# Row-tiled feed-forward products, a new order of the slot and two gates of eight on GpSimd, in a kernel of thresholded attention and a gated feed-forward layer

## The chip, the cores and the metric

The kernel runs on one core of one Trainium2 chip. The metric is the device time of one execution in microseconds (us). Before the change it is 562.9 us, the median of three runs (561.4 to 563.7).

The engines in the profile are PE (TensorE, matmuls), PEld (its weight loads), DVE (VectorE), ACT (ScalarE), POOL (GpSimd) and SP (DMA queues). A "q" behind an engine's name means its sequencer, the part that takes instructions in order.

## The reference

```python
# q, k, v: (8, 8, 576, 64) f32; w_in: (512, 2048); w_out: (2048, 512)
scores = scale * np.matmul(q, k.transpose(0, 1, 3, 2))
thresh = np.max(scores, axis=-1, keepdims=True) - tau
scores = np.where(scores >= thresh, scores, -1000000000.0)
...                                          # softmax of what is left: attn
x = np.matmul(attn, v)                       # then (4608, 512)
h = x @ w_in
g = h * np.clip(h + 3.0, 0.0, 6.0) / 6.0     # the gate
out = g @ w_out
```

## The kernel before

Sixteen groups of four heads are worked through in nine slots each, 144 slots in all. In a slot VectorE takes 128 rows of scores of two heads out of the accumulators and finds each row's maximum. GpSimd turns the maximum into a bias, ScalarE masks with that bias and later exponentiates, and GpSimd normalises. Between these stand pieces of the feed-forward layer of an earlier batch: an input product (512 to 2048 wide, two blocks of 128 at a time), its gate, and a quarter of an output product. The code below is condensed; `...` marks what is left out.

```python
    def sm_max(sl):
        ...
        for i, ps in enumerate(sl.tiles):
            nc.vector.tensor_scalar(out=sl.s[:, i, :]..., in0=ps[:, :, 0:HALF],
                                    scalar1=1.0, scalar2=None, op0=Alu.mult, op1=Alu.max,
                                    accum_out=sl.m[:, i:i + 1])
            nc.gpsimd.tensor_scalar(out=sl.bias[:, i:i + 1], in0=sl.m[:, i:i + 1], scalar1=-scale, scalar2=tau,
                                    op0=Alu.mult, op1=Alu.add)
    ...
    def sm_norm(sl):
        for i in range(2):
            nc.gpsimd.tensor_scalar(out=pn[:, i, :], in0=sl.s[:, i, :], scalar1=sl.rinv[:, i:i + 1], scalar2=1.0,
                                    op0=Alu.mult, op1=Alu.mult)
    ...
    def mm1(item, pool=None):                        # input product: full 128 rows
        for n in range(2):
            for ki in range(KI):
                nc.tensor.matmul(hps[:, n, 0:w], w_in_sb[:, ki, (ni + n) * P:(ni + n + 1) * P],
                                 xT[b][:, ki, c0:c0 + w], start=(ki == 0), stop=(ki == KI - 1))
    def mm1_relu(hps, on_act):                       # max(h + 3, 0), on ScalarE or VectorE
    def mm1_gate(item, hps, r):                      # min(r, 6) * h, on VectorE
    ...
    # one slot
        sm_exp(prev, 0); sm_exp(prev, 1)
        sm_max(sl)
        h = mm1(item)
        r = mm1_relu(h, on_act=(slot in (0, 1, 3, 5)))
        mm1_gate(item, h, r)
        ...                                          # a quarter of an output product
        sm_mask(sl, 0); sm_mask(sl, 1)
        ...                                          # transposes, or attention times values
        queue[n + 1].tiles = scores(...)             # the next slot's scores
        sm_norm(prev)
```

The input product has one pair of accumulator banks (`ps_h`, bufs=1). The gate of a slot frees it for the next slot's product.

Of the kernel before, what the change touches and what calls it, by code (L numbers as in the profile page):

```python
# [21 lines left out]
def kernel(  # L22
# [21 lines left out]
    N2 = 28  # L44
# [13 lines left out]
    r_pool = ctx.enter_context(tc.tile_pool(name="rp", bufs=2))  # L58
    g_pool = ctx.enter_context(tc.tile_pool(name="gp", bufs=1))
# [4 lines left out]
    ps_m = ctx.enter_context(tc.psum_pool(name="ps_m", bufs=1))  # L64
# [126 lines left out]
    def bank(name):  # L191
        nonlocal turn
        turn += 1
        if now < N2 and turn % 2:
            return ps_o.tile([P, 512], F32, tag="o", name=name)
        return ps_m.tile([P, 512], F32, tag="m", name=name)
# [12 lines left out]
    def main_pe(src, pair):  # L209
        ps = bank("tp")  # L210
        n = pair % 2
        for t in range(4):
            nc.tensor.transpose(ps[:, t * P:(t + 1) * P], src[:, t, 2 * n:2 * n + 2, :], identf[:])  # L213
        return ps

    def transpose_q(pair):
        nq = nat[pair // 2][0]
        if by_pe(pair):
            ps = main_pe(nq[:, 0:1024].rearrange("p (t h d) -> p t h d", h=4, t=4), pair)
            return lambda: nc.vector.tensor_copy(out=qT_of(pair)[:, 0:512], in_=ps[:])  # L220
        n = pair % 2
        nc.vector.transpose(out=qT_of(pair), in_=nq[:, n * S:(n + 1) * S])

    def transpose_k(pair):
        ps = main_pe(nat[pair // 2][1], pair)
        return lambda: copy_out(kT_of(pair)[:, 64:576], ps[:])

    def transpose_rest(quad):
        ps = bank("tr")
        nq, _, kr = nat[quad]  # L230
        nc.tensor.transpose(ps[:, 0:P], kr[:], identf[:])
        if by_pe(2 * quad):
            nc.tensor.transpose(ps[:, P:2 * P], nq[:, 1024:1152], identf[:])

        def evict():
            qT, kT = qkT[quad]
            both = ps[:].rearrange("p (w n t) -> p w n t", n=2, t=64)
            if by_pe(2 * quad):
                nc.vector.tensor_copy(out=qT[:, :, 512:S], in_=both[:, 1])
            copy_out(kT[0:64, :, S:S + 64], both[0:64, 0])  # L240
            copy_out(kT[64:P, :, 0:64], both[64:P, 0])
        return evict
# [7 lines left out]
    def scores(quad, slot):  # L250
        tiles = [ps_s.tile([P, 2, 512], F32, tag="s", name="s") for _ in range(2)]
        for hf in range(2):
            if slot < 8:
                pair, t = 2 * quad + slot // 4, slot % 4
                for a in range(2):
                    nc.tensor.matmul(tiles[a][:, hf, 0:HALF], qT_of(pair)[a * 64:(a + 1) * 64, t * P:(t + 1) * P],  # L256
                                     keys(pair, a, hf), start=True, stop=True)
            else:
                for n in range(2):
                    for a in range(2):  # L260
                        pair = 2 * quad + n
                        nc.tensor.matmul(tiles[a][n * 64:(n + 1) * 64, hf, 0:HALF],  # L262
                                         qT_of(pair)[a * 64:(a + 1) * 64, 512:S], keys(pair, a, hf),
                                         start=True, stop=True)
        return tiles
# [4 lines left out]
    def sm_max(sl):  # L270
        sl.s = s_pool.tile([P, 2, S], F32, tag="s", name="s")
        sl.m = stat_pool.tile([P, 2], F32, tag="m", name="m")
        sl.bias = stat_pool.tile([P, 2], F32, tag="bias", name="bias")
        sl.rsum = stat_pool.tile([P, 2], F32, tag="rsum", name="rsum")
        sl.rinv = stat_pool.tile([P, 2], F32, tag="rinv", name="rinv")
        for i, ps in enumerate(sl.tiles):
            nc.vector.tensor_scalar(out=sl.s[:, i, :].rearrange("p (a b) -> p a b", a=2), in0=ps[:, :, 0:HALF],  # L277
                                    scalar1=1.0, scalar2=None, op0=Alu.mult, op1=Alu.max,
                                    accum_out=sl.m[:, i:i + 1])
            nc.gpsimd.tensor_scalar(out=sl.bias[:, i:i + 1], in0=sl.m[:, i:i + 1], scalar1=-scale, scalar2=tau,  # L280
                                    op0=Alu.mult, op1=Alu.add)
# [36 lines left out]
    def av(ps, pair, pT, cols):  # L318
        b, hp = divmod(pair, NPAIR)
        vm, vr = vsb[b]  # L320
        for c in range(4):
            for a in range(2):
                nc.tensor.matmul(ps[a * 64:(a + 1) * 64, :], vm[:, 2 * hp + a, c * D:(c + 1) * D],  # L323
                                 pT[:, 5 * a + c, cols], start=(c == 0), stop=False)
# [3 lines left out]
    def av_main(pair):  # L328
# [3 lines left out]
        ps = bank("av")  # L332
        av(ps[:], pair, pts[pair], slice(0, 512))
        o0 = 64 if b % 2 else 0
        nc.vector.tensor_copy(out=xT[b][:, hp, o0:o0 + 512], in_=ps[:])  # L335

    def av_rest(quad):
        b, g = divmod(quad, 2)
        ps = bank("ar")
        for n in range(2):  # L340
            av(ps[:, n * 64:(n + 1) * 64], 2 * quad + n, ptr[quad], slice(n * 64, (n + 1) * 64))
        o0 = 0 if b % 2 else 512
        nc.vector.tensor_copy(out=xT[b][:, 2 * g:2 * g + 2, o0:o0 + 64],
                              in_=ps[:, 0:P].rearrange("p (a b) -> p a b", a=2))
# [3 lines left out]
    def mm1(item, pool=None):  # L348
# [6 lines left out]
        return hps[:, :, 0:w]  # L355

# [16 lines left out]
    o_ps = {}  # L373

    def mm2_part(bb, mt, part, pool=None):
        if part == 0:
            if pool:
                o_ps[0] = pool.tile([P, 2, 512], F32, tag="s", name="o")[:, 0, :]
            else:
                o_ps[0] = ps_o.tile([P, d_model], F32, tag="o", name="o")[:]  # L380
        for ni in range(part * 4, part * 4 + 4):
            nc.tensor.matmul(o_ps[0], gbuf[:, ni, mt * P:(mt + 1) * P], w_out_sb[:, ni, :],  # L382
                             start=(ni == 0), stop=(ni == NI - 1))

    def mm2_out(bb, mt, on_act):
        osb = o_pool.tile([P, d_model], F32, tag="osb", name="osb")
        if on_act:
            nc.scalar.activation(out=osb[:], in_=o_ps[0], func=Act.Copy, scale=1.0 / 6.0)  # L388
        else:
            nc.vector.tensor_scalar_mul(out=osb[:], in0=o_ps[0], scalar1=1.0 / 6.0)  # L390
# [16 lines left out]
    def moe_of(b):  # L407
        items = []
        for c0, w, mts in (((0, 320, (4, 5, 6)), (320, 256, (7, 8))) if b % 2 else
# [3 lines left out]
            items[-1] = (items[-1][0], [(b // 2, mt, part) for mt in mts for part in range(4)])  # L413
# [19 lines left out]
    prev = None  # L433
    for n, sl in enumerate(queue):
# [11 lines left out]
        if slot == 0 and g == 1 and b + 1 < B:  # L446
            load_v(b + 1)
        if prev is not None:
            for i in range(2):
                sm_exp(prev, i)  # L450
        sm_max(sl)

        if slot != 8 and todo1:
            item, then = todo1.pop(0)
            h = mm1(item)
            r = mm1_relu(h, on_act=(slot in (0, 1, 3, 5)))
            mm1_gate(item, h, r)
            todo2.extend(then)
        copies = pe_transpose(queue[n - 2]) if n > 1 and queue[n - 2].on_chip else None
        if prev is not None:  # L460
            sm_recip(prev)
        if copies:
            copies()
        outs = []


        pieces = 0 if slot == 3 else 1
        if slot == 0:
            second = True
        if second and slot < 2 and len(todo2) > 1 and todo2[0][1] == todo2[1][1]:  # L470
            pieces, second = 2, False
        for _ in range(pieces):
            if todo2:
                bb, mt, part = todo2.pop(0)
                mm2_part(bb, mt, part)
                if part == 3:
                    outs += mm2_out(bb, mt, on_act=False)
        for i in range(2):
            sm_mask(sl, i)
        evict = None  # L480
        nxt = 2 * quad + 2
        if slot == (1 if quad else 2):
            evict = transpose_q(2 * quad + 1)
        elif slot == (2 if quad else 3):
            evict = transpose_k(2 * quad + 1)
        elif slot == 3 and quad > 0:
            av_main(2 * quad - 1)
        elif slot == 4 and quad > 0:
            av_rest(quad - 1)
            if quad % 2 == 0:  # L490
                todo1.extend(moe_of(quad // 2 - 1))
        elif slot in (5, 6, 7) and quad + 1 < NQUAD:
            if slot == 5:
                alloc_qk(quad + 1)
                evict = transpose_q(nxt)
            elif slot == 6:
                evict = transpose_k(nxt)
            else:
                evict = transpose_rest(quad + 1)
        elif slot == 8:  # L500
            av_main(2 * quad)
        if evict:
            evict()
# [4 lines left out]
        if prev is not None:  # L508
            sm_norm(prev)
        flush()  # L510
# [23 lines left out]
    def rest2():  # L534
        while todo2:
            bb, mt, part = todo2.pop(0)
            mm2_part(bb, mt, part, pool=ps_s if count[1] % 3 else None)
            if part == 3:
                flush()
                late.extend(mm2_out(bb, mt, on_act=(count[1] % 2 == 0)))  # L540
                count[1] += 1
# [3 lines left out]
    av_main(2 * last + 1)  # L545
    rest2()
    av_rest(last)
# [38 lines left out]
```

## Time and profile before

| before | value | how to read it |
|---|---|---|
| time | 562.9 us | median of 3 runs |
| nine slots in the loop from slot 27 on | 31.5 us | from the starts of the row maxima, slots 36 to 135 |
| end of the loop to end of the program | 60 us | from the last slot's first maximum at 502.5 us |

The prediction below shows the main lines and the engines' shares in the loop. These are three more of the page's groups of instructions, which matter for the argument about GpSimd. The columns are line, engine, operation, names, shapes and count, then busy time in us and the mean ns of one, then the idle time before.

```profile
L298 POOL TENSOR_SCALAR pn<-s,rinv 128x576 bf16<-128x576 f32 x288 | 211.6, 745 | 133.5 <-issue 58.5
...
L280 POOL TENSOR_SCALAR bias<-m 128x1 f32<-128x1 f32 x288 | 54.4, 189 | 69.0 <-DVE s L277 48.2
...
L364 DVE TENSOR_SCALAR r<-h 128x512 f32<-128x512 f32 (+1 forms) x54 | 40.5, 751 | 0.0
```

The normalisation is the only large GpSimd operation. It takes 0.745 us for 576 elements a partition. On VectorE the add-and-maximum of the gate (L364) takes 0.75 us.

### The profile page before, as it was taken

To read this page: it belongs to the slowest core of one execution; us is meant where nothing else is said; L and a number is where in the kernel's file an instruction comes from. 1 tells how busy PE (TensorE), PEld (TensorE's weight loads), DVE (VectorE), ACT (ScalarE), POOL (GpSimd) and SP (SyncE) were. 2 spreads that over 40 slices of the span, in tenths; PEclk is the share of its full clock that TensorE was granted. 3 is DMA by queue.
4 is the path that set the end of the run, shared out by engine and by line. 5 is a ranking of instruction groups with operands and counts; after the bars stand their busy time and mean duration, and the time that the engine had idled before them with its cause. 6 is when DMAs were issued, how large, how long until landed. Compare 5 with 4: busy or idle time off the path is not lost.

```text
span 562.3 us, 11634 instructions
## 1 busy us (share of the span) xinstructions
PE 535.0 (95%) x3856; PEld 309.3 (55%) x3856; DVE 424.4 (75%) x1040; ACT 470.3 (84%) x999; POOL 305.2 (54%) x646
## 2 busy tenths in 40 slices
PE   7998798899999999999999999999999999999997
PEld 5665455455545565555555565655555565654663
DVE  3588787687878788787878798887978798883440
ACT  4799899798988999989898999899898999983540
POOL 1678878854556555655456555755556555561000
PEclk8899999899999999999999999999999999999999
DMA  5879999997689876978589867987699865453102
GB/s 110 135 110 166 162 160 184 207 148 144 112 159 153 151 153 127 208 139 155 114 150 170 159 137 146 174 160 146 127 137 175 167 124 117 101 109 86 38 20 75
DMA packets 286204, 77.52 MB, mean 138 GB/s; under 512 B 269248, under 2 KB 281536, under 8 KB 286144
## 3 DMA queue, kind: packets, MB, share of 16 engines
q1 hardware_dynamic: 268736, 67.86, 64.8%
q0 software_dynamic: 17408, 8.92, 13.7%
q8 instruction: 30, 0.49, 0.4%
q14 instruction: 30, 0.25, 0.2%
HBM read 36.70 MB, written 9.44 MB: 82 GB/s over the span
## 4 chain that ended last, share of the span: by engine, by line
PE 58%; DVE 11%; ACT 9%; issue 4%; POOL 1%; DMA 1%; SPq 1%; DVEq 0%; POOLq 0%
PE h L353 18%; PE o L382 17%; PE s L256 16%; DVE s L277 5%; ACT s L285 4%; PE av L323 3%; ACT s L290 3%; DVE g L370 2%; DVE r L364 2%; ACT r L362 2%; PE s L262 1%; PE tp L213 1%; PE ar L323 1%; DVE osb L390 1%; POOL pn L298 1%
## 5 line engine op out<-in xcount | busy, mean ns | idle before, releaser
L298 POOL TENSOR_SCALAR pn<-s,rinv 128x576 bf16<-128x576 f32 x288 | 211.6, 745 | 133.5 <-issue 58.5
L277 DVE TENSOR_SCALAR_CACHE_REDUCE s<-s 128x576 f32<-128x576 f32 x288 | 205.9, 752 | 44.9 <-PE s L256 35.2
L285 ACT ACTIVATE s<-s,bias 128x576 f32<-128x576 f32 x288 | 207.1, 766 | 36.8 <-POOL bias L280 35.7
L290 ACT ACTIVATE s<-s 128x576 f32<-128x576 f32 x288 | 192.7, 671 | 0.3
L256 PE MATMUL s<-kT,qT 64*128 64x288 f32 x1024 | 172.7, 435 | 5.4 <-DVE s L277 3.2
L353 PE MATMUL h<-xT,w_in_sb 128*128 128x320 bf16 (+1 forms) x1024 | 145.0, 287 | 5.5 <-DVE g L370 4.6
L382 PE MATMUL o<-w_out_sb,g 128*128 128x512 bf16 x576 | 140.9, 379 | 3.6 <-DVE osb L390 3.0
L353 PEld LDWEIGHTS <-w_in_sb 128*128 128x128 bf16 x1024 | 92.0, 97 | 68.4 <-issue 31.1
L256 PEld LDWEIGHTS s<-kT,qT 64*128 64x128 f32 x1024 | 94.8, 188 | 62.7 <-DVE s L277 24.9
L370 DVE SCALAR_TENSOR_TENSOR g<-r,h 128x512 bf16<-128x512 f32 (+1 forms) x128 | 96.4, 754 | 41.2 <-ACT r L362 39.3
L280 POOL TENSOR_SCALAR bias<-m 128x1 f32<-128x1 f32 x288 | 54.4, 189 | 69.0 <-DVE s L277 48.2
L382 PEld LDWEIGHTS <-g 128*128 128x128 bf16 x576 | 55.6, 98 | 58.2 <-issue 9.8
L362 ACT ACTIVATE r<-h,three 128x640 f32<-128x640 f32 (+1 forms) x74 | 54.4, 737 | 21.1 <-PE h L353 20.4
L290 ACT ACTIVATION_READ_ACCUMULATOR s<-s 128x1 f32 x288 | 54.2, 188 | 0.0
L364 DVE TENSOR_SCALAR r<-h 128x512 f32<-128x512 f32 (+1 forms) x54 | 40.5, 751 | 0.0
L390 DVE TENSOR_SCALAR osb<-o 128x512 f32<-128x512 f32 x31 | 21.0, 676 | 22.2 <-PE o L382 22.2
L323 PE MATMUL av<-pT,vm 128*64 128x512 bf16 x256 | 34.6, 392 | 2.0 <-ACT kT L203 2.0
L323 PEld LDWEIGHTS <-vm 128*64 128x64 bf16 x512 | 18.1, 111 | 25.2 <-issue 18.3
L293 DVE RECIPROCAL rinv<-rsum 128x2 f32<-128x2 f32 x144 | 23.0, 160 | 10.2 <-ACT s L290 9.5
L335 DVE CAST xT<-av 128x512 bf16<-128x512 f32 x32 | 21.8, 681 | 5.6 <-PE av L326 5.3
L277 DVE DVE_READ_ACCUMULATOR s<-s 128x1 f32 x288 | 23.9, 83 | 0.0
L388 ACT ACTIVATE osb<-o 128x512 f32<-128x512 f32 x5 | 3.0, 597 | 23.9 <-PE o L382 23.9
(42 smaller groups left out, 255.9 us busy)
## 6 DMA issues: line engine op xcount, KB each, us to landing
km<-in_k_dram SPq DMA_DIRECT2D x64, 128.0 KB, 3.0
out_dram<-osb SPq DMA_DIRECT2D x32, 256.0 KB, 2.4
nq<-in_q_dram SPq DMA_DIRECT2D x96, 72.0 KB, 2.7
vm<-in_v_dram POOLq DMA_DIRECT2D x16, 256.0 KB, 5.4
nq<-in_q_dram SPq DMA_DIRECT2D x16, 128.0 KB, 3.9
w_in_sb<-in_moe_w_in_dram POOLq DMA_DIRECT2D x16, 128.0 KB, 4.1
w_out_sb<-in_moe_w_out_dram POOLq DMA_DIRECT2D x16, 128.0 KB, 4.5
pT<-pn SPq DMA_TRANSPOSE x119, 3.4
```

What stands on the lines that cost most here:

```text
L256: nc.tensor.matmul(tiles[a][:, hf, 0:HALF], qT_of(pair)[a * 64:(a + 1) * 64, t * P:(t + 1) * P], keys(pair, a, hf), start=True, stop=True)
L277: nc.vector.tensor_scalar(out=sl.s[:, i, :].rearrange("p (a b) -> p a b", a=2), in0=ps[:, :, 0:HALF], scalar1=1.0, scalar2=None, op0=Alu.m ...
L280: nc.gpsimd.tensor_scalar(out=sl.bias[:, i:i + 1], in0=sl.m[:, i:i + 1], scalar1=-scale, scalar2=tau, op0=Alu.mult, op1=Alu.add)
L285: nc.scalar.activation(out=s, in_=s, func=Act.Prelu, bias=sl.bias[:, i:i + 1], scale=scale, alpha=REJECT)
L290: nc.scalar.activation(out=s, in_=s, func=Act.Exp, accum_out=sl.rsum[:, i:i + 1])
L298: nc.gpsimd.tensor_scalar(out=pn[:, i, :], in0=sl.s[:, i, :], scalar1=sl.rinv[:, i:i + 1], scalar2=1.0, op0=Alu.mult, op1=Alu.mult)
L323: nc.tensor.matmul(ps[a * 64:(a + 1) * 64, :], vm[:, 2 * hp + a, c * D:(c + 1) * D], pT[:, 5 * a + c, cols], start=(c == 0), stop=False)
L353: nc.tensor.matmul(hps[:, n, 0:w], w_in_sb[:, ki, (ni + n) * P:(ni + n + 1) * P], xT[b][:, ki, c0:c0 + w], start=(ki == 0), stop=(ki == KI ...
L362: nc.scalar.activation(out=r, in_=hps, func=Act.Relu, bias=three[:])
L364: nc.vector.tensor_scalar(out=r, in0=hps, scalar1=3.0, scalar2=0.0, op0=Alu.add, op1=Alu.max)
L370: nc.vector.scalar_tensor_tensor(out=gbuf[:, ni:ni + 2, c0:c0 + w], in0=r, scalar=6.0, in1=hps, op0=Alu.min, op1=Alu.mult)
L382: nc.tensor.matmul(o_ps[0], gbuf[:, ni, mt * P:(mt + 1) * P], w_out_sb[:, ni, :], start=(ni == 0), stop=(ni == NI - 1))
```

## The change

Its intent: from slot 27 on, the input and output products run as pairs of 64-row tiles, so that TensorE need not switch its tiling between them and the scores. The two tiles write two banks and exchange them halfway; a VectorE nop between the two phases keeps them apart. Keys of four heads are transposed in one slot, token tiles of the output are spread over six slots, and of the eight gates of a group GpSimd takes two and ScalarE's relu two. The cut-out is condensed, with comments added.

```diff
-    N2 = 28
+    N2 = 27
+    ACT_RELU, POOL_GATE = (3, 6), (2, 5)
-    ps_m = ctx.enter_context(tc.psum_pool(name="ps_m", bufs=1))
...
+    class Banks:
+        def products(self, phase, insts):
+            follows(insts[0], self)
+            if self.phase not in (None, phase):
+                relay = nc.vector.nop(nofuse=True)
+                tc.add_manual_dep(relay.ins, self.after.ins.name, SYNC, reason="end of a phase")
+                tc.add_manual_dep(insts[0].ins, relay.ins.name, SYNC, reason="next phase")
+            self.phase, self.after = phase, None
...
+    def mm1_phase(item, hps, phase):
+        for ki in range(KI):
+            for a in range(2):
+                n, c = a ^ phase, row_tile(a)
+                insts.append(nc.tensor.matmul(
+                    hps[:, n, 0:w], w_in_sb[c, ki, (ni + n) * P:(ni + n + 1) * P], xT[b][c, ki, c0:c0 + w],
+                    start=(phase == 0 and ki == 0), stop=(phase == 1 and ki == KI - 1)))
+        h_banks.products(phase, insts)
...
+    def mm1_gate_pool(item, hs):
+        nc.gpsimd.tensor_scalar(out=r, in0=hs, scalar1=3.0, scalar2=0.0, op0=Alu.add, op1=Alu.max)
+        nc.gpsimd.tensor_scalar(out=r, in0=r, scalar1=6.0, scalar2=1.0, op0=Alu.min, op1=Alu.mult)
+        nc.gpsimd.tensor_tensor(out=gbuf[:, ni:ni + 2, c0:c0 + w], in0=r, in1=hs, op=Alu.mult)
...
     # one slot, from slot 27 on
+            if phase or nis.stop < NI:
+                parts = [(one, phase, nis[:4]), (one, phase, nis[4:])]
+        sm_max(sl, 0)
+                mm1_phase(item, h, 0)
+                mm2_phase(*parts[0][0], *parts[0][1:])
+                mm1_phase(item, h, 1)
+                mm2_phase(*parts[1][0], *parts[1][1:])
         sm_exp(prev, 0); sm_exp(prev, 1)
+        sm_max(sl, 1)
+        sm_mask(sl, 0)
+            if slot in by[1]:
+                hs = mm1_copy(h)
+                gate = lambda: mm1_gate_pool(item, hs)
+            else:
+                mm1_gate(item, h, mm1_relu(h, on_act=slot in by[0]))
+        sm_mask(sl, 1)
...
         sm_norm(prev)
+        if gate:
+            gate()
```

The GpSimd gate is emitted at the end of its slot, so it stands in GpSimd's order directly ahead of the next slot's two biases.

## The prediction

> **What bounds the kernel now.** I read the page first: engine shares, slices, the chain of waits.
>
> ```profile
> PE 535.0 (95%) x3856; PEld 309.3 (55%) x3856; DVE 424.4 (75%) x1040; ACT 470.3 (84%) x999; POOL 305.2 (54%) x646
> ...
> PE   7998798899999999999999999999999999999997
> ...
> PE 58%; DVE 11%; ACT 9%; issue 4%; POOL 1%; DMA 1%; SPq 1%; DVEq 0%; POOLq 0%
> ```
>
> TensorE is busy nearly everywhere after the first sixth and carries most of the chain. The change touches the loop from slot 27 of 144 on, so next came the busy times of that stretch, then those of the tail:
>
> ```profile
> 98.60:501.10 402.50, 393.64 (x2887) 224.66 (x2886) 332.52 (x814) 364.88 (x787) 230.62 (x488) 1.00 0.83 147
> ...
> 520.00:540.00 20.00, 19.77 (x164) 14.28 (x163) 11.53 (x16) 11.71 (x16) 0.00 (x0) 1.00 0.08 28
> ```
>
> The columns are length, then PE, weight loads, DVE, ACT, POOL, clock, DMA. In the loop TensorE is at 98%, ACT at 91%, DVE at 83%, POOL at 57%. The tail (after 501 us, 61 us) is all TensorE and the change leaves its arithmetic alone. But a busy PE need not be streaming, so I looked at TensorE's timeline for one slot:
>
> ```profile
> 307.11 1.24 PE L256 MATMUL s<-kT,qT 64*128 64x288 f32 x8
> 308.38 1.03 PE L353 MATMUL h<-xT,w_in_sb 128*128 128x256 bf16 x8
> 309.25 1.03 PE L382 MATMUL o<-w_out_sb,g 128*128 128x512 bf16 x4
> 310.11 0.60 PE L213 MATMUL tp<-identf,km 128*128 128x128 f32 x4
> 310.64 1.24 PE L256 MATMUL s<-kT,qT 64*128 64x288 f32 x8
> ```
>
> Scores run in two 64-row tiles, everything else on 128 rows. From the starts of single matmuls in the trace (between 110 and 500 us) the steady rates are: a pair of score matmuls every 0.242 us, 0.109 or 0.136 us for an input product of 256 or 320 columns, 0.216 us for an output product, 0.109 us for a transpose. Around the scores these rates are broken. Going into them takes 0.309 us after an output product instead of 0.216, and their second pair follows 0.346 us after the first instead of 0.242, for its weights were not loaded ahead: about 0.19 us together. Leaving them takes 0.335 us (median; mean 0.374) instead of 0.242: about 0.13 us. So a round trip costs 0.32 us, nine times in a group of four heads.
>
> As a check: groups 5 to 14 start at 167.2 us and end at 481.1, 31.4 us each. Streaming is scores 8 x 4 x 0.242 + 4 x 0.242 = 8.7; input products 64 x 0.1225 = 7.8; output products 2.25 x 16 x 0.216 = 7.8; attention times values 10 x 0.216 + 0.3 = 2.5; transposes 9 x 0.109 = 1.0. Sum 27.8. Nine round trips add 2.9, three entries into the values' column tiles 0.3. That is 31.0 of 31.4: TensorE sets the pace, and tiling switches are 10% of it.
>
> The waits between engines show what stands close behind:
>
> ```profile
> DVE g L370 <- ACT r L362: 39.3, 72, 3.4
> ACT s L285 <- POOL bias L280: 35.7, 72, 1.9
> DVE s L277 <- PE s L256: 35.2, 53, 2.8
> ...
> PE h L353 <- DVE g L370: 4.6, 11, 0.7
> ```
>
> VectorE is the one that waits for the scores; TensorE waits for the gates only 4.6 us in all.
>
> **What the Trainium skill says.** "TensorEngine Tiling (Array Packing)", Tiling Modes, Key Properties: changing the tiling mode drains TensorE. The trace agrees (0.09 us extra into the scores, 0.09 out, before weights). The same page, Gotcha 1: different row tiles must not access one PSUM bank at the same time, and software has to see to it. That is the reason for the phases; no trace here shows it. "Perfetto Trace Analysis", Per-engine timelines: a sequencer-only instruction performs its wait in the sequencer, before the next is fetched. In the trace a VectorE event wait before the row maximum passes 0.035 to 0.042 us after the modelled end of the scores, and later ones follow only then. "GPSIMD Engine Reference", Elementwise: a two-input operation takes about 2.6 cycles an element.
>
> **The change, part by part, for one group of nine slots.**
>
> Row-tiled products. Each 128-row product becomes two 64-row ones that run beside each other into two banks, as the scores' pairs do, so I keep 0.109 and 0.136 us a pair and no gain in streaming. What goes is switching: slots 1 to 7 get their scores straight after row-tiled work (slot 8's own 64x64 scores, the last transposes and the values still switch). That is 7 x 0.19 = 1.3 us off; the seven departures would be 7 x 0.13 = 0.9 us more. Slot 4 now has values between two phases, +0.2.
>
> Phase waits. In phase 1 each row tile writes the bank that the other wrote in phase 0. Before it a VectorE nop must see the first foreign product after phase 0 finish, and TensorE waits for the nop. But the helper's remembered phase is never cleared for the input products: phase 0 of the next slot also differs from the last phase 1, so it gets a nop too, and that nop stands in VectorE's order behind the first row maximum, which waits for these very scores. So the input product cannot follow the scores directly. Counted from the last score pair's start: its end at 0.402, the event passes at 0.44, event and the maximum's two instructions about 0.14 (four such dispatches take 0.24 between two event waits), the nop some 0.05 (an estimate from event records of 0.02 to 0.05), back to TensorE 0.055 (an output bank's release at 315.436 to its matmul at 315.49), weights 0.096. Sum 0.78 against 0.242 streaming: 0.5 us of idle TensorE, where leaving used to cost 0.13. Eight slots with a product: 8 x 0.37 = +3.0. The phase-1 nop costs little: from the end of phase 0 it needs 0.27 (first product's latency) + 0.04 + 0.05 + 0.055 + 0.096 = 0.51, and four output pairs fill 0.44: +0.07 in five slots, +0.35. It also holds back the second row maximum by about 0.4 us, VectorE time that then presses on the next gate.
>
> Sum: -1.3 + 0.2 + 3.0 + 0.35 - 0.1 (one entry less for values) = +2.1 us a group, 13 groups: +28 us. Had the phase-0 nop been free, it would be -1.3 - 0.9 + 0.2 + 0.35 - 0.1 = -1.7, so -23 us.
>
> Keys in one slot. Eight transposes become 16 of 64 rows, two at a time: same time, no switch, counted above. Token tiles over six slots: the same products, in halves of 16 x 0.109 = 1.75 us; VectorE and ACT get uneven slots, which costs a little where a short slot follows.
>
> ACT and GpSimd. ACT loses two relus of four, 2 x 0.62 (start to start) = 1.2 us of some 28 us; VectorE trades two gates (0.67 each) for two copies of the same size. GpSimd gets two gates: two operations of about 0.745 us (the page's row for 576 elements) and one two-input at 576 x 2.6 / 1.2 GHz = 1.25 us, an estimate from the page, 2.7 us each. 57% becomes about 75%. The ACT relief is worth something only if TensorE stops being the bound.
>
> **Rivals.** (1) The switches were the bound and the waits hide: 27.8 us streaming, six switches left; ACT (26.7 us a group) and VectorE (25.5) come close behind, and 29 to 30 us a group would give 535 to 545 us. For it: the arithmetic of before closes with switches alone, and a change with so many matched parts has probably been tried out. Against it: the nop behind the row maximum. (2) The nop's idle time replaces the switches, 575 to 595 us, as summed. For it: VectorE demonstrably passes its wait only after the scores end. Against it: the gate of the slot before must free the bank anyway, about then (gates end 1.0 us into the next slot where VectorE does both steps), so part of the wait was there. (3) VectorE or GpSimd becomes the bound: nops block VectorE's order, and a 2.7 us gate ahead of the next bias delays the mask, 600 us and more. For it: ACT's 35.7 us of bias waits. Against: a slot's slack of GpSimd, 1.4 us, takes half of it up.
>
> **Range and chances.** The sum says 590, the free-nop case 540. I trust the nop's cost more from the order of instructions, but a kernel tuned this far was hardly built to idle; weighing 0.6 to 0.4 gives 570, a little more for uneven slots: 572. The range from 541 to 600 takes in both. Chances: faster 0.30, within 2% 0.30, slower 0.40.
>
> **What would show it.** Right: TensorE's busy share in the loop falls from 98%, input products wait for VectorE's sequencer once a slot for some 0.4 us, score pairs after row-tiled work follow at 0.242 from the first pair, groups take 33 us. Wrong: input products start 0.25 us after the last score pair, groups take 29 to 30 us, ACT over 93% busy; or bias waits several times 35.7 us, which would be rival 3. Unequal tails (61 us) would mean I misjudged where the work ends.

## The result, and the profile after

The changed kernel takes 764.1 us (median of 4 runs, 759.4 to 764.5), against 562.1 us (561.3 to 563.7) for the kernel before in the same rounds. The ratio is 1.357, with a 95% interval from 1.351 to 1.363. Ratios here are the mean time of one kernel's fast runs over the mean of the other's fast runs of the same rounds, so they are not quite the ratio of the medians quoted. The change costs 202 us; the range ended at 600. The outputs are right.

The page of the changed kernel, with the same parts as shown for the kernel before and the granted clock (PEclk) as well:

```profile
PE 579.5 (76%) x6088; PEld 391.5 (51%) x6088; DVE 434.6 (57%) x1041; ACT 460.6 (60%) x972; POOL 455.0 (60%) x724
...
PE   8997876766967776786776878679675797767897
...
PEclk7999997888979999888898899989799899988999
...
PE 38%; POOL 22%; DVE 14%; ACT 10%; issue 4%; DMA 1%; SPq 0%; POOLq 0%; DVEq 0%
```

No engine is busy more than 76% of the span. GpSimd, 1% of the chain of waits before, is 22% now, some 168 us. The slices of TensorE are no longer full, and its granted clock is lower in many of them.

The same windows as before, the loop and a stretch of the tail. The columns are length, PE, weight loads, DVE, ACT, POOL, clock, DMA share and GB/s:

```profile
98.60:701.00 602.40, 439.39 (x5156) 306.50 (x5157) 346.39 (x827) 360.61 (x771) 383.47 (x574) 0.87 0.57 101
720.00:740.00 20.00, 19.24 (x161) 14.06 (x160) 11.13 (x16) 11.63 (x16) 0.00 (x0) 1.00 0.07 27
```

Nearly the whole loss lies in the loop: 602 us instead of 403, with TensorE at 73% instead of 98%. In the profiled executions slot 27 starts (first row maximum) at 99.2 us here and at 93.8 before, so some 5 of the 202 us come earlier. That part goes with the execution rather than with the edit. Nearly all the kernels below that are built from the changed one have its code up to there (e4 has not). Where the clock granted in the first 20 us was 1.00, their slot 27 started at 92.9 to 93.2 us (e7, e10, e12, e14, e16); at 0.83 it was 95.7 to 97.0 (e5, e6, e9, e13, e15), at 0.76 to 0.77 it was 97.3 to 99.2 (the changed kernel, e1, e3, e11, e17). A step of a few us between two medians can be partly this; the table of steps has columns without it.

The tail is as it was. From the last slot's first maximum (702.3 us) to the end (762.7) are 60.4 us, against 59.8 before.

The waits between engines of the changed kernel (waited for in total, times, longest):

```profile
ACT s L336 <- POOL bias L331: 237.7, 140, 6.8
PEld L415 <- DVEq L222: 178.1, 98, 6.9
DVE g L433 <- ACT r L425: 162.1, 46, 7.6
POOL bias L331 <- DVE s L328: 150.6, 104, 11.2
...
PE h L415 <- DVE g L433: 148.3, 57, 8.4
```

ScalarE's mask waits 238 us for the bias, where it waited 36. VectorE's gate waits 162 us for ScalarE's relu, where it waited 39. TensorE's input product waits 148 us for VectorE's gate, where it waited 4.6. These rows overlap in time; they are three links of one chain. One stretch of the timeline shows the links (start, length, then in brackets the idle time before and what ended it):

```profile
394.13 2.36 POOL L447 TENSOR_SCALAR r<-hs 128x640 f32<-128x640 f32 x1
...
394.93 0.76 DVE L328 TENSOR_SCALAR_CACHE_REDUCE s<-s 128x576 f32<-128x576 f32 x1 [0.38 <-PE o L456]
...
396.58 2.36 POOL L448 TENSOR_SCALAR r<-r 128x640 f32<-128x640 f32 x1
399.02 1.53 POOL L449 TENSOR_TENSOR g<-r,hs 128x640 bf16<-128x640 f32 x1
400.50 0.70 POOL L127 DMA_DIRECT2D vr<-in_v_dram  x1
401.27 0.46 POOL L331 TENSOR_SCALAR bias<-m 128x1 f32<-128x1 f32 x2
401.49 0.77 ACT L336 ACTIVATE s<-s,bias 128x576 f32<-128x576 f32 x1 [6.76 <-POOL bias L331]
...
402.29 0.80 ACT L425 ACTIVATE r<-h,three 128x640 f32<-128x640 f32 x1
...
403.12 0.82 DVE L433 SCALAR_TENSOR_TENSOR g<-r,h 128x640 bf16<-128x640 f32 x1 [7.35 <-ACT r L425]
...
403.99 1.25 PE L415 MATMUL h<-xT,w_in_sb 64*128 64x320 bf16 x8 [6.95 <-DVE g L433]
```

The second row maximum of the slot is done by 395.7 us, but GpSimd is in the middle of the gate of the slot before (L447 to L449, then the start of a DMA). The biases are made only at 401.27. Then everything goes in order: mask, relu behind it, gate, and TensorE, which had been idle for 6.95 us. Three engines, ScalarE, VectorE and TensorE, stood still behind one GpSimd gate. Its durations, from the groups by shape (the first number behind the bar is the busy time in us, the second the mean ns of one):

```profile
L447 POOL TENSOR_SCALAR r<-hs 128x640 f32<-128x640 f32 x13 | 30.7, 2359 | 2.5 <-DVE hs L440 2.5
L448 POOL TENSOR_SCALAR r<-r 128x640 f32<-128x640 f32 x13 | 30.7, 2358 | 1.1
L447 POOL TENSOR_SCALAR r<-hs 128x512 f32<-128x512 f32 x13 | 25.1, 1932 | 0.9
L448 POOL TENSOR_SCALAR r<-r 128x512 f32<-128x512 f32 x13 | 25.1, 1931 | 1.1
L449 POOL TENSOR_TENSOR g<-r,hs 128x640 bf16<-128x640 f32 x13 | 19.9, 1532 | 1.1
L449 POOL TENSOR_TENSOR g<-r,hs 128x512 bf16<-128x512 f32 x13 | 16.4, 1263 | 1.1
```

A gate takes 2.36 + 2.36 + 1.53 = 6.2 us for 640 elements a partition and 5.1 us for 512, on average 5.7 us; 26 of them are 148 us.

### The profile page after: what moved, and what is told of

The parts are those of the page before. It is cut to its first block, busy times and chain, and to the rows that moved or that the text cites. A ratio compares the mean times of both kernels' runs of the same rounds, so it can differ in the third digit from the quotient of the medians.

```text
span 762.7 us, 16326 instructions
## 1 busy us (share of the span) xinstructions
PE 579.5 (76%) x6088; PEld 391.5 (51%) x6088; DVE 434.6 (57%) x1041; ACT 460.6 (60%) x972; POOL 455.0 (60%) x724
## 4 chain that ended last, share of the span: by engine, by line
PE 38%; POOL 22%; DVE 14%; ACT 10%; issue 4%; DMA 1%; SPq 0%; POOLq 0%; DVEq 0%
PE h L415 12%; POOL r L448 6%; POOL r L447 6%; DVE g L433 6%; PE o L456 6%; PE o L374 5%; ACT s L336 4%; POOL g L449 4%; PE o L463 4%; DVE r L427 3%; PE s L305 3%; PE s L312 3%; ACT r L425 3%; POOL pn L349 3%; PE h L405 3%
## 5 line engine op out<-in xcount | busy, mean ns | idle before, releaser
L336 ACT ACTIVATE s<-s,bias 128x576 f32<-128x576 f32 x288 | 215.3, 771 | 238.7 <-POOL bias L331 237.7
L415 PE MATMUL h<-xT,w_in_sb 64*128 64x256 bf16 (+1 forms) x1584 | 150.9, 314 | 156.0 <-DVE g L433 148.3
L415 PEld LDWEIGHTS <-w_in_sb 64*128 64x128 bf16 x1584 | 80.1, 101 | 209.9 <-DVEq L222 178.1
L456 PE MATMUL o<-w_out_sb,g 64*128 64x256 bf16 x1792 | 118.4, 269 | 0.0
L456 PEld LDWEIGHTS <-g 64*128 64x128 bf16 x1792 | 93.6, 94 | 7.7
L447 POOL TENSOR_SCALAR r<-hs 128x512 f32<-128x512 f32 (+1 forms) x26 | 55.8, 2145 | 3.5 <-DVE hs L440 2.5
L448 POOL TENSOR_SCALAR r<-r 128x512 f32<-128x512 f32 (+1 forms) x26 | 55.8, 2145 | 2.3
L374 PE MATMUL o<-pT,vm 128*64 128x512 bf16 x256 | 45.4, 489 | 0.3 <-DVE kT L237 0.3
L449 POOL TENSOR_TENSOR g<-r,hs 128x512 bf16<-128x512 f32 (+1 forms) x26 | 36.3, 1398 | 2.2
L405 PE MATMUL h<-xT,w_in_sb 128*128 128x256 bf16 (+1 forms) x232 | 31.5, 291 | 6.6 <-DVE g L433 5.6
L239 ACT COPY kT<-o 64x128 f32<-64x128 f32 (+1 forms) x55 | 21.9, 421 | 23.8 <-PE o L270 9.0
```

The lines of the kernel that those rows point to most:

```text
L336: nc.scalar.activation(out=s, in_=s, func=Act.Prelu, bias=sl.bias[:, i:i + 1], scale=scale, alpha=REJECT)
L374: inst = nc.tensor.matmul(ps[a * 64:(a + 1) * 64, :], vm[:, 2 * hp + a, c * D:(c + 1) * D], pT[:, 5 * a + c, cols], start=(c == 0), stop=F ...
L415: insts.append(nc.tensor.matmul(hps[:, n, 0:w], w_in_sb[c, ki, (ni + n) * P:(ni + n + 1) * P], xT[b][c, ki, c0:c0 + w], start=(phase == 0 ...
L447: nc.gpsimd.tensor_scalar(out=r, in0=hs, scalar1=3.0, scalar2=0.0, op0=Alu.add, op1=Alu.max)
L448: nc.gpsimd.tensor_scalar(out=r, in0=r, scalar1=6.0, scalar2=1.0, op0=Alu.min, op1=Alu.mult)
L449: nc.gpsimd.tensor_tensor(out=gbuf[:, ni:ni + 2, c0:c0 + w], in0=r, in1=hs, op=Alu.mult)
```

## The experiments

They are grouped by question. The edits are against the changed kernel unless the text says otherwise. The kernel before took 561.7 to 563.5 us (median).

### Is it the GpSimd gates, and are they enough alone?

**e1_no_pool_gate** takes the two gates off GpSimd; VectorE and ScalarE have them again.

```diff
-    ACT_RELU, POOL_GATE = (3, 6), (2, 5)
+    ACT_RELU, POOL_GATE = (2, 3, 5, 6), ()
```

> The changed kernel with no gate on GpSimd: slots 2, 3, 5 and 6 have ACT's relu and VectorE's gate, so the loads of ACT and VectorE are those of the kernel before; row tiles, phase waits, token tiles and keys stay as changed. Theory G (the 26 gates on GpSimd, 5.7 us each, stand ahead of the next slot's bias, so mask, relu and gate of that slot come 7 us late and TensorE with them): 570 to 600 us, and the waits of the mask for the bias fall from 238 us to under 60. Theory N (the nops on VectorE cost the time): still over 700 us.

Measured: 612.7 us (607.2 to 614.3), ratio to the kernel before 1.087 (1.081 to 1.092). So the gates cost 764.1 - 612.7 = 151 us, 5.8 us for each of the 26, about their whole duration. All else in the change costs 50 us. Theory G is right in kind, but both its numbers were missed by a little (600 us at most, mask waits under 60). The waits of this run:

```profile
PEld L415 <- DVEq L222: 80.8, 98, 1.5
DVE g L433 <- ACT r L425: 72.6, 72, 2.3
...
ACT s L336 <- POOL bias L331: 64.6, 109, 2.3
PE h L415 <- DVE g L433: 43.7, 66, 1.1
```

The mask's longest wait for a bias falls from 6.8 to 2.3 us. What is left is TensorE's wait for the nop (L222) and for the gate.

**e2_before_pool_gate** does the opposite: the kernel before, with only these two gates moved to GpSimd at the end of slots 2 and 5.

```diff
+            if n >= N2 and slot in (2, 5):
+                hs = mm1_copy(h)
+                gate = lambda item=item, hs=hs: mm1_gate_pool(item, hs)
+            else:
...
+        if gate:
+            gate()
```

> The kernel before with one part of the change alone: in slots 2 and 5 from slot 28 on, VectorE copies the product and GpSimd does the gate in three operations after the norm. No row tiles, no nops. Theory G: 26 gates at about 7 us each of late bias put the time at 700 to 770 us. Theory N: GpSimd has time to spare (54% busy), so 560 to 590 us.

Measured: 677.1 us (674.2 to 679.3), ratio 1.204 (1.200 to 1.209). The gates alone cost 115 us in a kernel without row tiles and nops, 4.4 us each. This is lower, and why a gate costs less here is not shown. The wait is the one of the theory, with the longest one as in the changed kernel:

```profile
ACT s L286 <- POOL bias L281: 154.5, 59, 6.7
```

### Why is one gate 5.7 us and not 2.7?

**e3_forms** puts other forms of the same GpSimd operation in place of the first two of a gate. In slot 2 these are multiply and add only, so the formula there is wrong on purpose. The output still passed the comparison, so that pass says nothing about this formula. In slot 5 the added constant comes from a per-partition operand in one, and the other writes bf16.

```diff
+        if slot == 2:
+            nc.gpsimd.tensor_scalar(out=r, in0=hs, scalar1=3.0, scalar2=1.0, op0=Alu.mult, op1=Alu.mult)
+            nc.gpsimd.tensor_scalar(out=r, in0=r, scalar1=3.0, scalar2=1.0, op0=Alu.add, op1=Alu.mult)
+        else:
+            nc.gpsimd.tensor_scalar(out=r, in0=hs, scalar1=three[:, 0:1], scalar2=0.0, op0=Alu.add, op1=Alu.max)
...
+            nc.gpsimd.tensor_scalar(out=rb, in0=r, scalar1=6.0, scalar2=1.0, op0=Alu.min, op1=Alu.mult)   # rb: bf16
```

> The changed kernel with other forms of the gate's two tensor-scalar operations on GpSimd, wrong on purpose in slot 2: there multiply by 3 and 1, then add 3 and multiply by 1, both f32 to f32; in slot 5 add and max with the 3 taken from a tile, then min and multiply written as bf16. My prediction took 0.745 us for each from the norm (multiply, multiply, per-partition scalar, bf16 out, 576 elements), and 2.15 us was measured. If max and min are what is slow, slot 2's two take 0.7 to 0.9 us and slot 5's 1.9 to 2.4. If it is f32 output, slot 5's second falls to 0.8 and slot 2's stay at 2. If it is scalars that are constants, slot 5's first falls and the others stay.

Measured: 714.7 us. The groups by shape:

```profile
L451 POOL TENSOR_SCALAR r<-hs,three 128x640 f32<-128x640 f32 x7 | 17.0, 2431 | 2.6 <-DVE hs L440 2.6
L453 POOL TENSOR_SCALAR rb<-r 128x640 bf16<-128x640 f32 x7 | 16.5, 2362 | 0.6
...
L448 POOL TENSOR_SCALAR r<-hs 128x640 f32<-128x640 f32 x6 | 4.4, 727 | 0.0
L449 POOL TENSOR_SCALAR r<-r 128x640 f32<-128x640 f32 x6 | 4.4, 726 | 0.5
```

Multiply and add take 0.73 us for 640 elements; the forms with a maximum or a minimum take 2.4 us, whether the constant is immediate or an operand and whether the result is f32 or bf16. The maximum and the minimum are what is slow in these operations: (2.359 - 1.932) us / 128 elements = 3.3 ns an element. The run as a whole was 49 us shorter than the changed kernel, with 39 us less GpSimd work (415.8 against 455.0 us); as a single look this only points the same way as e1.

### Is it the amount of GpSimd work or its place?

**e7_gate_spread** leaves all three operations of each gate on GpSimd, one at the end of each of three slots.

```diff
-            gate()
+            gate_steps.extend(gate())
+        if gate_steps:
+            gate_steps.pop(0)()
```

> The changed kernel with its gates on GpSimd, but the three operations of a gate spread over three slots, one after each slot's norm: the same work on GpSimd, no bias behind more than one operation of 2.4 us. Theory G by order (biases wait behind 5.7 us): the 151 us that the gates cost against e1 shrink to a quarter or less, 620 to 650 us. Theory G by amount of work on GpSimd: no less than 720 us.

Measured: 637.8 us (633.5 to 642.7), ratio 1.134 (1.128 to 1.141). Its page and waits:

```profile
PE 532.0 (84%) x6085; PEld 366.9 (58%) x6088; DVE 432.3 (68%) x1041; ACT 457.6 (72%) x972; POOL 454.9 (72%) x724
...
ACT s L336 <- POOL bias L331: 123.5, 129, 3.0
```

GpSimd does the same 455 us of work as in the changed kernel, yet 126 of the 151 us are gone. So the amount of work is not what costs. A piece still stands ahead of the biases in each of three slots; what costs is the uninterrupted 5.7 us in one place.

**e4_bias_dve** was to take the biases out from behind the gates by giving them to VectorE.

```diff
-        nc.gpsimd.tensor_scalar(out=sl.bias[:, i:i + 1], in0=sl.m[:, i:i + 1], scalar1=-scale, scalar2=tau,
+        nc.vector.tensor_scalar(out=sl.bias[:, i:i + 1], in0=sl.m[:, i:i + 1], scalar1=-scale, scalar2=tau,
```

> The changed kernel with the bias (one element a partition) computed by VectorE instead of GpSimd, so that no mask waits behind a gate; the gates on GpSimd stay as long as they are. Theory G in its form 'order': 570 to 630 us and mask waits for the bias under 60 us. Theory G in its form 'throughput' (GpSimd simply has too much work): GpSimd is at 60% of 763 us, 455 us, so this is ruled out unless the time stays over 700. Theory N: over 700 us.

Measured: 683.4 us (682.7 to 685.2), ratio 1.216 (1.214 to 1.219). This is inconclusive for the question. The waits of some 7 us behind the gates are gone, but a new cost came in: the bias now stands between the first maximum and the nop, and waits for that maximum to finish, so the nop comes about 0.7 us later in every slot. TensorE then waits for VectorE's sequencer 163 us in 98 times, twice the 81 us of e1. The run leaves the question to e7.

**e10_relu_moved** leaves the gates and moves ScalarE's relu out of the slots behind them.

```diff
-    ACT_RELU, POOL_GATE = (3, 6), (2, 5)
+    ACT_RELU, POOL_GATE = (1, 4), (2, 5)
```

> The changed kernel with ACT's two relus in slots 1 and 4 in place of 3 and 6, the slots right behind the GpSimd gates, whose relu VectorE then does. Theory C (the way from a late bias to TensorE goes through ACT's order: mask, then relu, then VectorE's gate and the free bank): 640 to 700 us, and VectorE's wait for ACT's relu falls from 162 us to under 40. Rival (the late mask and exp hold VectorE's reciprocal a slot later just as long): 740 to 765 us.

Measured: 711.5 us (707.2 to 712.8), ratio 1.262 (1.253 to 1.271). The time lies between the two expected ranges. The link through the relu is worth 52 us, and the waits suggest that another took its place: VectorE's gate waits 26.5 us for ScalarE's relu instead of 162, and its reciprocal waits 102 us for the exponentials, which stand behind the late masks in ScalarE's order.

### What are the other 50 us?

**e5_no_first_nop** is e1 without the nop ahead of phase 0 of the input product.

```diff
-    ACT_RELU, POOL_GATE = (3, 6), (2, 5)
+    ACT_RELU, POOL_GATE = (2, 3, 5, 6), ()
...
+                h_banks.phase = None
                 mm1_phase(item, h, 0)
```

> The kernel without GpSimd gates (e1, 612.7 us) and also without the nop ahead of phase 0 of the input product: its bank pair was read out by the gate of the slot before, which the product waits for anyhow. Theory N (that nop, queued behind the first row maximum, keeps TensorE idle 0.4 us a slot and VectorE's second maximum with it): 40 to 55 us less than e1, 558 to 573 us, level with the kernel before. Rival H (h has one buffer: the gate of the slot before frees it at about the same time, so the wait only changes its name): 600 to 613 us.

Measured: 601.5 us (600.9 to 605.2), ratio 1.071 (1.067 to 1.075): 11 us less than e1, of which the profiled executions show 6 from slot 27 on. From the starts of single matmuls, the step from the last score to the input product is still 0.67 us on average, for now it waits for the gate of the slot before, which frees its banks. TensorE's waits for that gate are 41.8 us and 38.2 us (matmul and weight load; the two can overlap).

```profile
PE h L415 <- DVE g L433: 41.8, 68, 1.0
```

**e6_nop_before_max** is e1 with that nop kept, but the first maximum emitted behind it.

```diff
-        if late_slot:
...
+        if late_slot and not (item and (parts or small)):
             sm_max(sl, 0)
...
                 mm1_phase(item, h, 0)
+                sm_max(sl, 0)
```

> e1 with the same nops, but the first row maximum emitted after phase 0 of the input product, so that the phase-0 nop stands ahead of the maximum in VectorE's order and need not wait for the scores. Theory N (it is the place in the order, not the nop): as without the nop, 558 to 578 us. Rival H: 600 to 613 us. If nops themselves cost (105 of them in the loop at some 0.1 us), e6 is 10 us above e5.

Measured: 607.1 us (603.3 to 609.3), ratio 1.078 (1.072 to 1.083): 6 us less than e1, of which 3 from slot 27 on. The intervals of the two ratios overlap, so this is hardly more than noise; it is small, as in e5.

**e8_before_nop** measures the nop by itself: the kernel before, with a VectorE nop between the two maxima of each slot from 28 on, for which the input product waits.

```diff
+            if i == 1 and now >= N2:
+                sl.relay = nc.vector.nop(nofuse=True)
+                tc.add_manual_dep(sl.relay.ins, last_score[0].ins.name, SYNC, reason="end of the scores")
...
+                if relay is not None and n == 0 and ki == 0:
+                    tc.add_manual_dep(inst.ins, relay.ins.name, SYNC, reason="nop first")
```

> The kernel before plus one nop a slot from slot 28 on: it stands on VectorE between the two row maxima, waits for the slot's last score product, and the input product waits for it. No row tiles. Theory N: 0.3 to 0.45 us in each of about 104 slots, 593 to 610 us. Rival H: the gate of the slot before sets the input product's start anyway, 562 to 572 us.

Measured: 589.3 us (588.7 to 592.7), ratio 1.049 (1.045 to 1.053). That is 27 us, 0.26 us in each of some 103 slots. This nop waits for the slot's last score, while that of the change stands behind the maximum that waits for it. The mechanism is real in a kernel where TensorE waits for little else; its size is 0.7 of the 0.37 us in the prediction, just under the range for this run.

```profile
PEld L360 <- DVEq L282: 75.9, 103, 1.1
```

**e9_split_early** is e5 with the second phase of the input product always after four output pairs. In the changed kernel up to three slots of nine (0, 2 and 5) have 16 pairs between the phases.

```diff
-            if phase or nis.stop < NI:
+            if True:
                 parts = [(one, phase, nis[:4]), (one, phase, nis[4:])]
```

> e5 (no GpSimd gates, no phase-0 nop, 601.5 us) with phase 1 of the input product always after four output pairs; in e5 a slot with a whole phase 0 of an output tile puts 1.75 us of output products between the two halves. Theory H (the one input bank pair is the loop: half 1 late, relu, gate, then the next product; TensorE idles 0.5 to 0.8 us after the scores behind such slots, of which there are some 32): 15 to 30 us less than e5, 572 to 587 us, and the wait of the input product for VectorE's gate falls from 80 us to under 45. Rival S (row tiles themselves stream slower, or the uneven slots cost it): 597 to 603 us.

Measured: 585.9 us (583.4 to 587.8), ratio 1.040 (1.034 to 1.046): 15.5 us less than e5, and 20 from slot 27 on in the profiled executions. With the product finished earlier, its gate is earlier, and TensorE waits for gates 28.1 + 31.6 us instead of 41.8 + 38.2. The time is in the expected range; the waits, 60 us together, are not (under 45).

```profile
PE h L415 <- DVE g L433: 28.1, 49, 1.0
```

**e11_outputs_first** is e9 with some output pairs ahead of phase 0, so that the input product comes when its banks are free.

```diff
-                mm1_phase(item, h, 0)
-            if parts:
-                mm2_phase(*parts[0][0], *parts[0][1:])
...
+            fill.pop(0)()               # four output pairs, or the slot's transposes or values
+            sm_max(sl, 0)
...
+                mm1_phase(item, h, 0)
+                if fill:
+                    fill.pop(0)()
+                mm1_phase(item, h, 1)
```

> e9 (585.9 us) with TensorE's order in a slot changed so that other work stands between the scores and phase 0 of the input product: four output pairs (or the first of the values and key jobs), then phase 0, four output pairs, phase 1, the rest. The first part comes before the first row maximum in VectorE's order. Theory H: the 28 us that TensorE idles after the scores for the gate of the slot before fall to under 10 us, and as the switches stay away the time is 545 to 568 us, level with or under the kernel before. Rival S (VectorE and ACT set the slots by now): 577 to 588 us.

Measured: 606.1 us (604.4 to 610.2), ratio 1.079 (1.074 to 1.083): 20 us more than e9, so this expectation fell. From the starts in the trace, VectorE's second maximum follows the first after 1.14 us (median; longest 2.38) where it was 0.69 in e9 (longest 1.14), for the nop of phase 1 comes later in the slot. That this is the whole of the 20 us is not shown.

**e12_outputs_first_relu4** is e11 with ScalarE's relu in slot 4 instead of slot 3.

```diff
-    ACT_RELU, POOL_GATE = (2, 3, 5, 6), ()
+    ACT_RELU, POOL_GATE = (2, 4, 5, 6), ()
```

> e11 with ACT's relu in slot 4 instead of slot 3, since VectorE reads out the values in slot 4. If VectorE's order is what is left over in that slot, 3 to 10 us less than e11; if TensorE is the bound again, within 3 us of it.

Measured: 595.8 us (591.5 to 596.3), ratio 1.057 (1.052 to 1.062): 10 us less than e11, from the place of one relu.

### What are the last 24 us, and do the row tiles pay?

**e13_both_max_first** is e9 with both maxima ahead of the nops.

```diff
             sm_max(sl, 0)
+            sm_max(sl, 1)
...
-        sm_max(sl, 1)
```

> The best row-tiled version so far (e9_split_early, 585.9 us) with VectorE's second row maximum emitted directly behind the first, ahead of the waiting instruction of the second phase. Theory H2 (the rest over the kernel before, 24 us, is VectorE's second maximum held behind the second phase's waiting instruction, and the chain behind it): the maximum no longer waits, 565 to 578 us. Theory S (the rest is TensorE standing at the switches of phase and of row tiling, whatever VectorE does): 583 us or more, and TensorE's waits for VectorE's queue grow, as the second waiting instruction now comes behind one more operation.

Measured: 582.8 us (579.8 to 583.6), ratio 1.033 (1.030 to 1.036): 3 us less than e9, within the noise (the intervals of the ratios overlap). The maximum held behind the nop is not the rest.

**e14_both_max_relu4** is e13 with the relu moved as in e12.

```diff
-    ACT_RELU, POOL_GATE = (2, 3, 5, 6), ()
+    ACT_RELU, POOL_GATE = (2, 4, 5, 6), ()
```

> As e13_both_max_first, with ScalarE's relu in slots 2, 4, 5, 6 instead of 2, 3, 5, 6. If VectorE's gate waiting for the relu of slot 3 still bounds the stretch there, 5 to 12 us under e13 (the same step gave 10 us from e11 to e12); if not, within 4 us of it.

Measured: 575.1 us (574.4 to 580.7), ratio 1.023 (1.018 to 1.028). This has the lowest median of the versions with row tiles. It is still slower than the kernel before, clear of noise, though at the limit of 2% the verdict is unclear.

**e15_no_row_tiles** is e9 with the row tiles and nops taken out of both products and the order, the banks and the keys left.

```diff
-                h_banks.phase = None
-                mm1_phase(item, h, 0)
+                h = mm1(item)
...
-                    obank[:, j, 0:DH], gbuf[c, ni, mt * P:(mt + 1) * P], w_out_sb[c, ni, j * DH:(j + 1) * DH],
+            nc.tensor.matmul(obank[:, phase, 0:DH], gbuf[:, ni, mt * P:(mt + 1) * P],
+                             w_out_sb[:, ni, phase * DH:(phase + 1) * DH], start=(ni == 0), stop=(ni == NI - 1))
```

> e9_split_early with the row tiles and their waiting instructions taken out of the two products: the input product in full rows, the output product in full rows with one half of the columns in each phase, in the same places of the same order; keys, banks, order of the maxima and all else as in e9. Theory N (the waits on VectorE between the phases cost more than the row tiles save): under e9 by 10 to 25 us, 560 to 576. Theory O (the changed order of the slot and the fewer accumulator banks cost the rest; the row tiles pay for themselves): 590 us or more, as the switches come back, about 0.4 us a slot of 113.

Measured: 609.2 us (604.3 to 610.3), ratio 1.078 (1.073 to 1.083): 23 us more than e9. So within the new order the row tiles with their nops do pay, and it is the rest of the change, without them and without the GpSimd gates, that costs 46 us against the kernel before. No run has the row tiles in the old order. The edit also joins the two halves of the input product, so the 23 us is not the switches alone.

**e16_relu_even** and **e17_relu_first** look for the last 12 us in ScalarE's order. Both are e14; the one has its relu in every second slot, the other has the relu ahead of the slot's first mask.

```diff
-    ACT_RELU, POOL_GATE = (2, 4, 5, 6), ()
+    ACT_RELU, POOL_GATE = (0, 2, 4, 6), ()      # e16
```

```diff
+        if late_slot and item and slot in ACT_RELU:      # e17
+            r = mm1_relu(h, on_act=True)
         if late_slot:
             sm_mask(sl, 0)
```

> e14_both_max_relu4 with ScalarE's relu in slots 0, 2, 4, 6 instead of 2, 4, 5, 6: every second slot. If ScalarE's and VectorE's shares of the gates still set the step of a slot, as from e13 to e14 (8 us), this even spread gives 3 to 10 us more, 565 to 572; if TensorE's own order is the bound by now, within 4 us of e14 (575).

> e14_both_max_relu4 with ScalarE's relu emitted ahead of the first mask of its slot, not behind it, as the kernel before has it. VectorE's gate waits for the relu 57 us in all in e14; if the mask ahead of the relu is the reason and it bounds the slot, 5 to 15 us under e14 (560 to 570); if the masks then come later by as much and the exponentials behind them bound the slot, within 4 us of e14 or over it.

Measured: e16 582.7 us (578.6 to 586.1), ratio 1.038 (1.034 to 1.042); e17 576.1 us (573.7 to 577.1), ratio 1.024 (1.020 to 1.027). The even spread is 8 us worse than e14 (4 from slot 27 on), and the relu ahead of the mask leaves it where it was. Neither is the rest.

The steps, as the time of nine slots (from the starts of the row maxima of slots 36 and 135, divided by 11), as the time from slot 27 to the end (both from the one profiled execution) and as the whole:

| kernel | nine slots, us | slot 27 to end, us | median, us |
|---|---|---|---|
| before | 31.5 | 468.5 | 562 |
| changed | 46.6 | 663.5 | 764 |
| e1: no GpSimd gates | 35.1 | 513.5 | 613 |
| e5: also no first nop | 34.6 | 507.8 | 601 |
| e9: also second phase early | 33.0 | 488.1 | 586 |
| e13: also both maxima first | 32.9 | 485.7 | 583 |
| e14: also relu moved | 32.4 | 479.8 | 575 |
| e15: e9 without row tiles | 34.9 | 511.5 | 609 |

## Why the prediction was wrong

The number, 572 us, and the range to 600 us were wrong by far. The price and the place of the GpSimd gates are most of it (151 us). Without them the change still takes 613 us (e1), where the prediction's sum was 590. Taking the prediction's steps in order:

- **What bounds the kernel before**: right. TensorE's order set the pace, and e8 confirms it from the other side: 0.26 us put before the input product in each slot came out as 27 us at the end.
- **Row-tiled products**: right in rate, and the size fits. In the changed kernel a pair of 256 columns still streams in 0.109 us. The step from an output product to the scores takes 0.105 us where it took 0.309. The prediction put the whole with a free nop at -23 us; the difference between e15 and e9 is 23 us. That the two agree so closely is partly luck: e15 changes more than the switches, and e9 has other waits than the sum. What the prediction missed is that this gain does not show against the kernel before, because the new order of the slot costs more (46 us in e15).
- **The nop of phase 0**: the mechanism was right, the size too high. The prediction had +3.0 us a group, 39 us in all. Taking that nop away gave 11 us (e5), or 6 from slot 27 on. The objection written beside rival 2, that the gate of the slot before must free the bank at about that time anyway, is what the trace of e5 shows.
- **The nop of phase 1, "+0.07 in five slots"**: undersized. The working assumed four output pairs between the phases everywhere, while in up to three slots 16 stand there. Putting four everywhere gave 15.5 us (e9), or 20 from slot 27 on. This cost is not the nop's latency: the input product ends late, its gate is late, and so is the release of the banks.
- **"ACT and GpSimd"**: this is the step that failed. It said "two operations of about 0.745 us (the page's row for 576 elements)" and "2.7 us each". The row was of a multiplication; the gate's operations have a maximum and a minimum, and took 1.93 and 2.36 us (e3: 0.62 and 0.73 us without them). The gate is 5.7 us. The estimate for the two-input operation, 1.25 us for 576 elements, was near, if a little low: 1.26 us for 512 and 1.53 us for 640.
- **Rival 3** was named and is what happened; it was dismissed with "a slot's slack of GpSimd, 1.4 us, takes half of it up". Two things were wrong with that. The gate was twice as long. And the slack is an average, while the gate stands in one piece ahead of a bias, and mask, relu, VectorE's gate and TensorE all stand in line behind that bias. With the same work in three pieces 126 of 151 us are back (e7). The sign the prediction gave for rival 3, bias waits "several times 35.7", is there: 237.7 us.
- **"The ACT relief is worth something only if TensorE stops being the bound"**: no gain from it shows. TensorE did stop being the bound, but ScalarE was at 60%, standing behind GpSimd; no run isolates the relief.
- **Token tiles over six slots, "which costs a little where a short slot follows"**: probably undersized, but not settled. The order of the slot, the banks and the uneven pieces together cost 46 us without row tiles (e15), and some 24 us with them in e9. Moves of a relu and a maximum took 11 us of that (e13, e14). In e14 the trace shows TensorE idle for 21 us in 49 gaps between the scores and the input product, against 3.4 us in 14 gaps before; there it waits for the gate of the slot before. That the fewer banks and the uneven output pieces make that gate late is argued, not shown. The last 11 to 12 us stay open.
- **The tail**: right, equal to within a microsecond.

The lower granted clock in the changed kernel's loop (0.87) goes along with TensorE's idle time; the runs do not separate a share of the loss for it. In e14, where TensorE waits little, the trace has 1.00 between 110 and 500 us, as before the change.

## What to carry to other kernels

Take an operation's price from a row with the same arithmetic on the same engine, not from a row of the same size: minimum and maximum against multiply made a factor of three here. Before moving work to an engine with slack, ask which small operation stands behind it in that engine's order and who waits for that one; a gate of 5.7 us in one piece cost 4.4 us (e2) to 5.8 us (e1) there, and the same work cut in three cost about 1 us (25 us for 26 gates, e7). When a change has many matched parts, run it once with each part alone: here the row tiles saved 23 us within the new order (e9 against e15), while that order cost 46 us and the two gates on GpSimd 151. Compare small steps from the stretch that was edited, not from whole times: the first 95 us alone differed by 6 us between executions.

## What the Trainium skill lacked or had wrong

- "GPSIMD Engine Reference", Engine selection, calls one-input elementwise work, with max among its examples, roughly line-rate on GpSimd. A one-input operation with a maximum or a minimum took 1.93 us for 512 elements a partition and 2.36 us for 640 (3.3 ns an element), against 0.62 and 0.73 us for multiply and add (0.8 ns an element). Its two-input figure (Elementwise, about 2.6 cycles; at the page's 1.2 GHz an estimate of 2.2 ns) held: (1.532 - 1.263) us / 128 = 2.1 ns an element.
- "TensorEngine Tiling (Array Packing)", Tiling Modes, Key Properties, says that a change of mode drains TensorE, but gives no price. Here the step from an output product to the scores took 0.309 us across a change of mode, where the product streams at 0.216, and 0.105 us without a change, at the rate of the pairs. Without row tiles the best comparable kernel was 23 us slower (e15 against e9).
- No page gives the price of a nop that passes a wait from TensorE through VectorE back to TensorE. Put ahead of one product a slot, it cost 0.26 us each time (e8).
